# Seven block products in the first chunk's channel product, w_out's first pieces at fixed places, and split weight halves

## The chip, the cores and the metric

The kernel runs on one core of a Trainium2 chip. The metric is the device time of one execution in microseconds (us). The engines are named as the profile names them: PE multiplies matrices, PEld loads its weights, ACT (ScalarE), DVE (VectorE) and POOL (GpSimd) work element by element, SP issues the transfers.

## The reference

Three layers are computed one after the other. The weights come as 64-bit floats, q, k and v as 32-bit ones.

```python
# attention, B 4, H 8, S 576, D 64, window 64
scores = scale * np.matmul(q, k.transpose(0, 1, 3, 2))
mask = (rel >= 0) & (rel < window)
attn = exp(scores - max); attn = attn / (attn.sum + 1e-09)
x = (attn @ v), heads joined: [4, 576, 512]
# gated layer
h = np.maximum(x @ w_in, 0.0)
u, v = (h[..., :512], h[..., 512:])
v_s = np.einsum('ts,bsd->btd', w_spatial, layernorm(v)) + b_spatial[None, :, None]
x = (u * v_s) @ w_out
# mixing layer
h = np.maximum(x.transpose(0, 2, 1) @ w_tok1, 0.0) @ w_tok2
u = x + h.transpose(0, 2, 1)
h2 = np.maximum(u @ w_ch1, 0.0) @ w_ch2      # 512 -> 1536 -> 512
return u + h2
```

## The kernel before

**Number format.** Every product is made of three matmuls on 32-bit words that are split in a high and a low part: high by high, high by low, low by high (`mm3`, L155; the two helpers that make the parts are `split`, L147: a cast on ACT, line L148, and a subtraction, on DVE or POOL, line L149). A 64-bit weight first becomes a 32-bit word: ACT scales its upper half (`down`, L72), and DVE puts the bits together in `to_f32` (L63, then L68 and L69). Words that come by `split_steps` have their cast at L101 and their low part at L103.

**Stages.** First attention and x @ w_in, in 18 steps (n = 0 to 17), written out in a fixed order for all engines (`manual_schedule`). After it the order of the program is chosen by a scheduler from the code's order and from priorities. Behind attention come the spatial product and `wout` (five pieces), `x2nat`, `tok1` and `tok2` (four batches), and between them the preparation of the channel weights: `load_c1(j)` and `load_c2(j)`, j = 0 to 5, each of which turns 128 x 1024 words to high and low parts. Both also make sums of blocks on POOL: `load_c1` writes them to the DRAM tile `sums`, `load_c2` splits its sums and writes all parts to the DRAM tile `scr`. They are put off by priority, and their transfers go out in the order of the list `sources`.

**The channel products.** The 2304 tokens go in three chunks of 768, each as two halves of 384. The first product of a chunk makes the rows j = 0 to 5 of u @ w_ch1 (two blocks of 128 rows, for two halves of tokens). In chunk 0 `ch1` does it plainly: 48 matmuls of 128 x 384 a row, 288 in all, with the casts `uh` and low parts `ul` of u. In chunks 1 and 2 `ch1_seven` takes seven products of half the depth, 42 matmuls a row. These need the four sums of a weight row (read back from `sums`, cast to `sh`, low part `sl`: `load_sums`) and four differences of token blocks t1 to t4 (`usums`, each a DVE subtraction at L771, a cast and a low part, laid in words that are no longer used). The sums of the seven products are put together on DVE (x, z, H) and relu'd on ACT. The second product is seven times `product` (12 matmuls for each of three transferred pieces `w<-scr`). Each takes a cast `oh` on ACT (L898) and a low part `ol` on DVE (L899) for each of its six blocks, and adds its result to U (L936, L947).

Of the kernel before, what the change touches and what calls it, by code (L numbers as in the profile page):

```python
# [10 lines left out]
F32R = mybir.dt.float32r  # L11
# [9 lines left out]
P = 128  # L21
NTOK = B * S
SCALE = 0.125
WN = 256
# [11 lines left out]
def tile_kernel(ctx, tc, qT, kT, kE, v, w_in, wsT, b_sp, w_out, w_t1, w_t2, w_c1, w_c2, outT):  # L36
# [37 lines left out]
    def split_steps(hi, lo, src, rows=P, dup=False, raw=None, val=None, eng=nc.vector):  # L74
# [14 lines left out]
        if wide:  # L89
            r3 = raw[:, :cols].rearrange("p (n w) -> p n w", w=2)  # L90
            low, high = r3[:tot, :, 0], r3[:tot, :, 1]
            if val is None:
                val = stage.tile([P, WN], F32, tag="val", name="val", bufs=2)
            x = val[:tot, :n]
            down(x, high)
            yield
            to_f32(x, [(low, high)])
            yield
        else:
            val = raw  # L100
        nc.scalar.copy(out=hi[:tot], in_=val[:tot, :n])  # L101
        yield
# [356 lines left out]
    def wv_part(k):  # L459
        return w_part(U[:, k, 1152:2176], w_in[128 * k:128 * k + 128, 512:].unsqueeze(1), wi_h[:, k:k + 1, 512:], wi_l[:, k:k + 1, 512:], 512)  # L460

    E = mybir.EngineType
    with tc.manual_schedule(engines={E.PE, E.SP, E.Activation, E.DVE, E.Pool}):
# [61 lines left out]
        uv_v(*its[0])  # L525
        conv, late = {1: (0,), 2: (1, 2), 3: (3,)}, ()
        ws_at = {2: 2, 3: 2, 4: 3, 5: 3}
        for n in range(1, len(its)):
# [10 lines left out]
            go(*cv[:1])  # L539
            go(*cv[:1])  # L540
            if some:
                sexp(n + 1, 0)
                sexp(n + 1, 1)
                snorm(n + 1)
# [14 lines left out]
            while work and left > 0:  # L559
                left -= run_work(1)  # L560
                tick()
            load_ws(ws_at.get(n, 0))
            enable(n)
        while turns:
# [13 lines left out]
    psA = pool("psA", bufs=5, space=PSUM)  # L578
    for k in range(4):
        load_cols(wo_h[:, k, :], wo_l[:, k, :], w_out[128 * k:128 * k + 128, :])  # L580
    while any(w[0] is not spatial for w in work):
# [12 lines left out]
    def c2_source(j):  # L594
# [6 lines left out]
    sources += [(c1_source(j) if w == 1 else c2_source(j), {}) for w, j in  # L601
                ((2, 0), (1, 0), (2, 1), (2, 2), (1, 1), (1, 2), (2, 3), (1, 3), (2, 4), (1, 4), (1, 5), (2, 5))]
    issued = []
# [150 lines left out]
    def usums(c, u):  # L754
# [18 lines left out]
        return [[(h[:, k], l[:, k]) for k in range(2)] for h, l in [(uh[:, :2], ul[:, :2]), (uh[:, 2:], ul[:, 2:]), (vh[:, 2:], vl[:, 2:])] + homes]  # L773

# [30 lines left out]
    tok1(3)  # L805
    load_c2(4)
    tok2(2)
# [29 lines left out]

    def ch1_seven(X):

        x11, x21, x22, t1, t2, t3, t4 = X  # L840
        S = [load_sums(j) for j in range(2)]
        outs, left = [], []
        for j in range(NJ):
            if j and j + 1 < NJ:
                S.append(load_sums(j + 1))
            s1, s2, s3, s4 = S[j]
            a, c = [psmm.tile([P, 512], F32, tag="mm", name="mm")[:, :HW] for _ in range(2)]
# [32 lines left out]
            left = [last]  # L880
            outs.append((h11, h12, h21, h22, e))
        left[0]()
        return [list(x) for x in zip(*outs)]

# [27 lines left out]
    for c in range(NTOK // TW):  # L912
        t0 = TW * c
        u = u[:1] if c == 0 else []
        u += [uin(c, h) for h in range(len(u), 2)]
        if c:
            b11, b12, b21, b22, e = ch1_seven(usums(c, u))
        else:
            b11, b12, b21, b22, e = [], [], [], [], []
            for j in range(NJ):  # L920
                if j == 0:
                    load_c1(5)
                    load_c2(5)
                x, y = ch1(u, j)
                b11.append(x)
                b12.append(y)
                x, y = ch1(u, j + NJ)
                b21.append(x)
                b22.append(y)
                e.append(diff(H(), b12[j], b11[j], nc.vector))  # L930
                diff(b12[j], b22[j], b12[j], nc.vector)
        us = [[U[:, 2 * dh:2 * dh + 2, t0 + HW * h:t0 + HW * h + HW] for h in range(2)] for dh in range(2)]
# [119 lines left out]
```

## Time and profile before

| | |
|---|---|
| median of 3 runs | 638.32 us (637.96 to 638.89) |
| profiled execution | 638.47 us |
| its span | 636.7 us, 12004 instructions |
| PE busy | 610.3 us, 96% of the span |
| DVE, ACT, POOL busy | 459.5, 334.1 and 153.4 us |
| granted clock | 1.00 |

The profiled execution took 1.8 us more than its span, and 0.15 us more than the median. The stages in the trace: attention to about 215 us, then the spatial product, the token mixing and the preparation of weights to 363.5 us, then three chunks, whose first ends near 454 us and whose second near 550 us. A row of the trace gives the start, the duration, the engine, the line, the operation, and in square brackets how long the engine stood idle ahead of it and what ended that.

### The profile page before, as it was taken

What the parts mean: (1) busy time and instruction counts of PE and PEld (TensorE: products, weight loads), DVE (VectorE), ACT (ScalarE), POOL (GpSimd) and SP (SyncE); (2) the same over time, 40 slices, a digit from 0 to 9 for tenths busy, and PEclk for the clock granted to TensorE, in tenths of its full rate; (3) what the DMA queues carried; (4) which work ended last, traced back from release to release, by engine and by line L of the source; (5) the groups of instructions that cost most, each with busy time, mean ns of one, the idle gap of its engine ahead of it and who ended that gap; (6) DMA issues with size and microseconds to landing.
All of it is one profiled execution on the core that took longest, in us unless ns stands there. A gap on an engine that the chain in (4) does not pass through costs nothing.

```text
span 636.7 us, 12004 instructions
## 1 busy us (share of the span) xinstructions
PE 610.3 (96%) x4455; PEld 566.8 (89%) x4455; DVE 459.5 (72%) x977; ACT 334.1 (52%) x839; POOL 153.4 (24%) x166
## 2 busy tenths in 40 slices
PE   5889999999999999999899999999999999999997
PEld 2568798998889899888788899999999999999987
DVE  4896857556584688769978951278875998867982
ACT  4777853545674464666554442345543646344550
POOL 5610000100010010565475471041000440002510
PEclk9999999999999999999999999999999999999999
DMA  8853473222330135557756455057433675534772
GB/s 325 271 158 112 152 235 127 78 77 75 102 116 2 34 118 158 177 193 248 256 183 218 183 174 218 0 198 257 149 125 133 220 230 196 178 103 151 255 248 75
DMA packets 46106, 103.60 MB, mean 163 GB/s; under 512 B 4192, under 2 KB 16736, under 8 KB 46048
## 3 DMA queue, kind: packets, MB, share of 16 engines
q1 hardware_dynamic: 46048, 102.84, 48.3%
q8 instruction: 35, 0.57, 0.4%
q14 instruction: 23, 0.19, 0.1%
HBM read 83.95 MB, written 18.87 MB: 162 GB/s over the span
## 4 chain that ended last, share of the span: by engine, by line
PE 64%; DVE 14%; ACT 7%; DMA 5%; issue 4%; POOL 3%; SPq 1%; DVEq 0%; ACTq 0%; POOLq 0%
PE mm L161 27%; PE A L904 17%; PE mm L833 8%; PE A L833 6%; ACT pb L264 3%; DMA U<-in_w_in 3%; POOL k L738 2%; DVE k L68 2%; DVE k L69 2%; PE xo L297 2%; PE pt L285 2%; DMA scr<-hl 2%; DVE k L63 1%; PE A L161 1%; PE sc L241 1%
## 5 line engine op out<-in xcount | busy, mean ns | idle before, releaser
L904 PE MATMUL A<-oh,w 128*128 128x384 f32 x480 | 102.7, 334 | 0.0
L886 POOL TENSOR_TENSOR H<-H 128x384 f32<-128x384 f32 x36 | 45.0, 1264 | 184.9 <-DVE ol L899 171.0
L899 DVE TENSOR_TENSOR ol<-H,oh 128x384 fp32r<-128x384 f32 x120 | 77.2, 676 | 16.4 <-ACT oh L898 12.7
L904 PEld LDWEIGHTS A<-oh,w 128*128 128x128 f32 x480 | 85.0, 188 | 0.0
L898 ACT CAST oh<-H 128x384 fp32r<-128x384 f32 x120 | 60.0, 514 | 41.5 <-PE A L904 31.0
L904 PE MATMUL A<-ol,w 128*128 128x384 f32 x240 | 61.4, 336 | 2.2 <-DVE ol L899 2.2
L161 PE MATMUL mm<-ws,nh 128*128 128x288 f32 x320 | 62.0, 297 | 0.4 <-DVE tmp L394 0.4
L161 PEld LDWEIGHTS mm<-ws,nh 128*128 128x128 f32 x320 | 49.9, 188 | 1.0 <-DVE tmp L394 0.6
L363 POOL TENSOR_SCALAR rstd<-mv 128x1 f32<-128x1 f32 x18 | 4.9, 272 | 178.4 <-DVE mv L362 178.3
L904 PEld LDWEIGHTS A<-ol,w 128*128 128x128 f32 x240 | 43.1, 188 | 3.3 <-DVE ol L899 3.2
L886 DVE TENSOR_TENSOR H<-H 128x384 f32<-128x384 f32 x36 | 22.6, 628 | 21.8 <-ACT H L826 19.6
L161 PE MATMUL mm<-ws,nl 128*128 128x288 f32 x128 | 37.7, 295 | 0.0
L264 ACT ACTIVATE pb<-pb,nm 128x128 f32<-128x128 f32 x96 | 37.3, 400 | 0.4 <-DVE nm L255 0.4
L286 ACT COPY PT<-pt 128x512 f32<-128x512 f32 x36 | 19.4, 591 | 31.5 <-PE pt L285 31.5
L272 DVE TENSOR_SCALAR rs<-sm 128x8 f32<-128x8 f32 (+1 forms) x19 | 3.3, 172 | 42.9 <-ACT pb L264 42.9
L161 PE MATMUL mm<-xh,wi_h 128*128 128x384 f32 x96 | 32.7, 341 | 0.7 <-ACT vf L357 0.6
L161 PE MATMUL mm<-xh,wi_l 128*128 128x384 f32 x96 | 32.1, 334 | 0.0
L161 PE MATMUL mm<-xl,wi_h 128*128 128x384 f32 x96 | 32.1, 334 | 0.0
L161 PE MATMUL mm<-gh,wo_h 128*128 128x512 f32 (+1 forms) x80 | 29.4, 378 | 0.1
L161 PE MATMUL mm<-gh,wo_l 128*128 128x512 f32 (+1 forms) x80 | 29.4, 370 | 0.0
L161 PE MATMUL mm<-gl,wo_h 128*128 128x512 f32 (+1 forms) x80 | 29.4, 370 | 0.0
L149 POOL TENSOR_TENSOR hl<-k,hl 128x512 fp32r<-128x512 f32 (+1 forms) x24 | 28.6, 1208 | 0.0
(190 smaller groups left out, 1691.4 us busy)
## 6 DMA issues: line engine op xcount, KB each, us to landing
w<-scr SPq DMA_DIRECT2D x63, 512.0 KB, 4.4
k<-in_w_c SPq DMA_DIRECT2D x24, 512.0 KB, 5.3
scr<-hl SPq DMA_DIRECT2D x18, 512.0 KB, 6.1
kk<-in_kT SPq DMA_DIRECT2D x16, 384.0 KB, 4.7
k<-sums SPq DMA_DIRECT2D x12, 512.0 KB, 3.2
qq<-in_qT SPq DMA_DIRECT2D x18, 256.0 KB, 4.0
va<-in_v SPq DMA_DIRECT2D x18, 256.0 KB, 2.9
vb<-in_v SPq DMA_DIRECT2D x18, 256.0 KB, 3.9
```

The lines of the kernel that those rows point to most:

```text
L68: nc.vector.scalar_tensor_tensor(out=y, in0=high, scalar=-0x80000000, in1=y, op0=ALU.bitwise_and, op1=ALU.bitwise_or)
L69: nc.vector.scalar_tensor_tensor(out=y, in0=low, scalar=29, in1=y, op0=ALU.logical_shift_right, op1=ALU.bitwise_or)
L149: eng.tensor_tensor(out=lo, in0=x, in1=f(hi), op=ALU.subtract)
L161: nc.tensor.matmul(o, a, c, start=(i == 0), stop=(i == n - 1))
L264: nc.scalar.activation(out=pb[:, h, :], in_=scs[g][:, h - 4 * g, :] if mk is None else pb[:, h, :], func=AF.Exp, scale=SCALE if mk is None ...
L285: nc.tensor.transpose(pt[:, h, :], pb[:, 4 * g + h, :], ident)
L286: nc.scalar.copy(out=PT[:, 4 * g:4 * g + 4, :], in_=pt)
L833: nc.tensor.matmul(o, a, m, start=first and i == 0, stop=i == len(todo) - 1, skip_group_check=True)
L886: eng.tensor_tensor(out=out, in0=a, in1=b, op=ALU.subtract)
L898: nc.scalar.copy(out=oh, in_=blk[j])
L899: nc.vector.tensor_tensor(out=ol, in0=blk[j], in1=f(oh), op=ALU.subtract)
L904: nc.tensor.matmul(acc[d], a, m, start=(first and j == 0 and i == 0), stop=(last and j == NJ - 1 and i == 2), skip_group_check=True)
```

## The change

It has five parts.

1. The first two of w_out's eight pieces get fixed places in attention: transfers at the end of step n = 11, the scaling on ACT at the end of n = 12, the six DVE operations of both in n = 14. Their casts and low parts, like the other six pieces, stay behind attention. Before, the scheduler placed all of it.
2. `load_c1` makes high and low part of its 1024 columns in two halves of 512.
3. The order of the last weights: all of W_ch1 ahead of W_ch2's fourth and fifth row; `load_c2(4)` and `load_c2(5)` stand in chunk 0 behind its first row, where only `load_c2(5)` stood.
4. `usums` makes t1 and t2 first, and t3 and t4 at a second call; the words in which they lie are exchanged among them.
5. Chunk 0 makes its rows j = 0 and 1 plainly (`ch1_four`), then rows 3, 4, 5 and 2 by seven products. t1 and t2 are made behind row 0; t3 and t4 behind the first two reads of sums. In chunks 1 and 2 the two reads come between t2 and t3.

```diff
+        if callable(hi):
+            hi, lo = hi()
...
+    def wo_part(i):
+        k, c = i // 2, WN * (i % 2)
+        return split_steps(lambda: [w[:, k, c:c + WN] for w in wo], None, w_out[128 * k:128 * k + 128, c:c + WN])
...
+        wo_open = [wo_part(i) for i in range(2)]
...
+            if n == 14:
+                go(*wo_open)
...
+            if n in (11, 12):
+                go(*wo_open)
...
-                ((2, 0), (1, 0), (2, 1), (2, 2), (1, 1), (1, 2), (2, 3), (1, 3), (2, 4), (1, 4), (1, 5), (2, 5))]
+                ((2, 0), (1, 0), (2, 1), (2, 2), (1, 1), (1, 2), (2, 3), (1, 3), (1, 4), (1, 5), (2, 4), (2, 5))]
...
-        split(both[:, :1024], both[:, 1024:], x)
+        for i in (0, 512):
+            split(both[:, i:i + 512], both[:, 1024 + i:1536 + i], x[:, i:i + 512])
...
-        homes = [(thirds(vh[:, :2]), thirds(vl[:, :2])), (apart(0, ws), apart(1, ws)), (apart(0, c1b), apart(1, c1b)),
-                 tuple(thirds(tq.tile([P, 2, HW], F32R, tag=n, name=n)) for n in ("th", "tl"))]
+        homes = [(apart(0, c1b), apart(1, c1b)), tuple(thirds(tq.tile([P, 2, HW], F32R, tag=n, name=n)) for n in ("th", "tl")),
+                 (apart(0, ws), apart(1, ws)), (thirds(vh[:, :2]), thirds(vl[:, :2]))]
...
-        for i, o, a, b in ((0, t1, x12, x11), (1, t2, x22, t1), (2, t3, x22, x12), (3, t4, x21, t2)):
+        for i, o, a, b in ((0, t1, x12, x11), (1, t2, x22, t1)):
...
+        yield
+        for i, o, a, b in ((2, t3, x22, x12), (3, t4, x21, t2)):
...
-    load_c2(4)
...
-    def ch1(u, ft):
+    def ch1(u, j):
...
-        for uh, ul in u:
+        for (uh, ul), ft in [(x, ft) for x in u for ft in (j, j + NJ)]:
...
+    def ch1_four(u, j):
+
+        x, z, y, w = ch1(u, j)
+        e = diff(H(), y, x, nc.vector)
+        return x, diff(y, w, y, nc.vector), z, w, e
+
+    def ch1_all(u, parts, plain):
+
+        outs, left = {}, []
+        seven_js = [j for j in (*range(NJ // 2, NJ), *range(NJ // 2))] if plain else list(range(NJ))
+        seven_js = [j for j in seven_js if j >= plain]
+        for j in range(plain):
+            if j == 0:
+                load_c1(5)
+            else:
+                load_c2(4)
+                load_c2(5)
+            outs[j] = ch1_four(u, j)
+            if j == 0:
+                next(parts)
+        if not plain:
+            next(parts)
+        S = {j: load_sums(j) for j in seven_js[:2]}
+        x11, x21, x22, t1, t2, t3, t4 = next(parts)
...
+        b11, b12, b21, b22, e = ch1_all(u, usums(c, u), 0 if c else 2)
```

What this does to the order of the instructions is seen at three places. In the rows of the order, the number behind L is the line of the kernel whose order it is; the changed kernel's lines from 101 on stand 2 to 38 further down.

**Attention, step n = 14.** DVE, before: vf is the normalised v of an earlier step, rs and pb are the division of the softmax, whose result PE transposes next.

```order
L366 TENSOR_SCALAR vf<-vf,mv,rstd 128x512
L272 TENSOR_SCALAR rs<-sm 128x8
L273 RECIPROCAL rs<-rs 128x8
L274 TENSOR_TENSOR pb<-pb,rs 128x1024
L335 TENSOR_TENSOR nl<-vf,nh 128x512
```

DVE in the changed kernel, at the same place, and below it ACT some steps ahead, where PT is the copy of the transposed softmax that the attention's second product takes (both with `val`, w_out's words).

```order
L368 TENSOR_SCALAR vf<-vf,mv,rstd 128x512
L63 TENSOR_SCALAR val<-val 128x256
L68 SCALAR_TENSOR_TENSOR val<-raw,val 128x256
L69 SCALAR_TENSOR_TENSOR val<-raw,val 128x256
L63 TENSOR_SCALAR val<-val 128x256
L68 SCALAR_TENSOR_TENSOR val<-raw,val 128x256
L69 SCALAR_TENSOR_TENSOR val<-raw,val 128x256
L274 TENSOR_SCALAR rs<-sm 128x8
L275 RECIPROCAL rs<-rs 128x8
L276 TENSOR_TENSOR pb<-pb,rs 128x1024
```

```order
L331 ACTIVATE U<-mm 128x256
L72 ACTIVATE val<-raw 128x256 x2
L288 COPY PT<-pt 128x512 x2
L266 ACTIVATE pb,sm<-pb,nm 128x128 x8
```

The six operations on val have moved in between vf and rs, and the two on ACT in between U and PT; before, both stood some six steps earlier.

**The transfers of chunk 0.** SP, before: `sums<-k` writes the block sums of W_ch1, `scr<-hl` the parts of W_ch2, `w<-scr` reads the weights of the second product.

```order
L717 DMA sums<-k_4583 128x1024
L742 DMA scr<-hl 128x512
L894 DMA w<-scr 128x1024 x3
L742 DMA scr<-hl 128x2x512
L894 DMA w<-scr 128x1024
L742 DMA scr<-hl 128x2x512 x2
L894 DMA w<-scr 128x1024 x13
```

SP in the changed kernel: `k<-sums` reads the block sums back (k_4768 is row j = 3, k_4774 row 4); the first five of the `scr` writes are those of `load_c2(4)` and the start of `load_c2(5)`.

```order
L733 DMA sums<-k_4562 128x1024
L134 DMA k_4652<-in_w_c 128x1024
L134 DMA k_4654<-in_w_c 128x1024
L758 DMA scr<-hl 128x512
L758 DMA scr<-hl 128x2x512 x3
L758 DMA scr<-hl 128x512
L758 DMA scr<-hl 128x2x512
L738 DMA k_4768<-sums 128x1024
L758 DMA scr<-hl 128x2x512 x2
L738 DMA k_4774<-sums 128x1024
L738 DMA k_4843<-sums 128x1024
L932 DMA w<-scr 128x1024 x17
```

The first read of sums has come to stand behind the second `scr` write of `load_c2(5)`, the second read behind its last.

**From the plain rows to the seven products.** ACT in the changed kernel, from the last parts of `load_c2(5)` (k_4677) on: `H<-mm` are the relus of the plain rows, p the copies of a first product, ws the high part of t3 (k_4635).

```order
L150 CAST hl<-k_4677 128x2x256
L845 ACTIVATE H<-mm 128x384 x2
L150 CAST sh<-k_4768 128x1024
L891 COPY p_4799<-mm 128x384
L891 COPY p_4862<-mm 128x384
L900 ACTIVATE H<-mm 128x384
L150 CAST sh<-k_4774 128x1024
L150 CAST ws<-k_4635 128x2x3x128
```

DVE in the changed kernel at the same place: `sl` are low parts of sums, k_4635 and k_4636 are t3 and t4, `ws` is the low part of t3.

```order
L151 TENSOR_TENSOR sl<-k_4768,sh 128x1024
L896 TENSOR_TENSOR x<-A,p_4799 128x384
L898 TENSOR_TENSOR z<-mm,p_4799 128x384
L151 TENSOR_TENSOR sl<-k_4774,sh 128x1024
L791 TENSOR_TENSOR k_4635<-U 128x768
L791 TENSOR_TENSOR k_4636<-U,k_4634 128x768
L896 TENSOR_TENSOR x<-A,p_4862 128x384
L151 TENSOR_TENSOR ws<-k_4635,ws 128x2x3x128
```

PE's rows at this place are 6 matmuls `uh,c1b`, 4 that need `sh`, 12 `uh,c1b`, 8 of which the first needs `sl`, 6 `uh,c1b`, and 18 on the sums of rows 3 and 4, then those on t3. None of these rows stands in the kernel before, where ACT and DVE have the relus and differences of plain rows 2 to 5 here.

## Rows read from the trace of the kernel before

**Rows 1.** PE's waits over the whole span: total us, times, longest.

```profile
PE pt L285 <- DVE pb L274: 5.7, 8, 1.2
...
PE A L904 <- DVE ol L899: 2.2, 3, 1.1
...
PE mm L161 <- ACT U L648: 1.4, 1, 1.4
...
PE mm L161 <- DVE hl L672: 0.7, 1, 0.7
PE mm L161 <- ACT uh L148: 0.7, 1, 0.7
...
PE mm L161 <- DVE U L683: 0.6, 1, 0.6
...
PE mm L161 <- DVE tmp L394: 0.4, 1, 0.4
```

**Rows 2.** Busy time by stretch: chunk 0's first product, chunk 1's.

```profile
364.00:411.70 47.70, 47.70 (x276) 47.67 (x276) 15.21 (x22) 16.50 (x34) 14.47 (x13) 1.00 0.39 138
...
454.00:496.00 42.00, 42.00 (x244) 42.00 (x244) 29.79 (x52) 17.22 (x32) 0.46 (x1) 1.00 0.45 154
```

**Rows 3.** The chain that ended last: start, us, engine, count.

```profile
363.53 48.17 PE mm L161 x276
...
465.09 1.04 PE mm L833 x6
```

**Rows 4.** Timeline of attention: ACT's val pair, steps before and in n = 14.

```profile
90.99 0.78 ACT L72 ACTIVATE val<-raw 128x256 f32<-128x256 f32 x2
...
174.53 1.06 PE L285 MATMUL pt<-ident,pb 128*128 128x128 f32 x8 [0.78 <-DVE pb L274]
...
179.39 0.17 DVE L272 TENSOR_SCALAR rs<-sm 128x8 f32<-128x8 f32 x1 [1.46 <-ACT pb L264]
```

**Rows 5.** Instructions on the tile val: ns minimum, median, maximum.

```profile
L63 DVE TENSOR_SCALAR val<-val x8: 286/293/294, 91.5 to 226.0; 128x256 int32<-128x256 int32 x8
L68 DVE SCALAR_TENSOR_TENSOR val<-raw,val x8: 414/420/427, 93.4 to 227.4; 128x256 int32<-128x256 int32 x8
```

**Rows 6.** Timeline of the stretch before 304.33 us, DVE and ACT.

```profile
301.47 0.68 DVE L69 SCALAR_TENSOR_TENSOR k<-k,k 128x512 int32<-128x512 int32 x1
...
302.19 1.05 ACT L148 CAST ws<-k 128x1024 fp32r<-128x1024 f32 x1 [2.68 <-DVE k L69]
...
303.27 1.52 DVE L149 TENSOR_TENSOR ws<-k,ws 128x1024 fp32r<-128x1024 f32 x1 [0.39 <-ACT ws L148]
...
303.70 0.57 ACT L648 COPY U<-mm 128x512 f32<-128x512 f32 x1
```

**Rows 7.** Timeline of ACT in tok2 of the second batch.

```profile
325.40 1.24 ACT L72 ACTIVATE k<-k 128x512 f32<-128x512 f32 x2 [0.69 <-POOL hl L149]
```

**Rows 8.** Timeline of W_ch2's last row in chunk 0, DVE and POOL.

```profile
368.31 1.28 DVE L69 SCALAR_TENSOR_TENSOR k<-k,k 128x512 int32<-128x512 int32 x2
...
373.69 1.29 POOL L149 TENSOR_TENSOR hl<-k,hl 128x512 fp32r<-128x512 f32 x1
```

**Rows 9.** Transfers of the tile sums, us from issue to landing (minimum, median, maximum).

```profile
DMA to landing us min/median/max: 2.6/3.3/4.6
```

**Rows 10.** POOL's block sums of W_ch2: ns minimum, median, maximum.

```profile
L738 POOL TENSOR_TENSOR k<-k x12: 733/1088/1387, 257.4 to 370.2; 128x256 f32<-128x256 f32 x12
```

**Rows 11.** Groups of instructions from 411 to 520 us: busy us, mean ns of one.

```profile
L149 DVE TENSOR_TENSOR sl<-k,sh 128x1024 fp32r<-128x1024 f32 x6 | 7.3, 1222 | 2.0 <-ACT sh L148 1.7 <-PE mm L833 0.3
L148 ACT CAST sh<-k 128x1024 fp32r<-128x1024 f32 x6 | 6.3, 1053 | 9.4 <-DMA k<-sums 8.1 <-DVE H L886 0.9 <-DVE ol L899 0.4
...
L858 DVE TENSOR_TENSOR x<-A,p 128x384 f32<-128x384 f32 x6 | 3.3, 556 | 4.3 <-ACT p L853 2.3 <-PE A L833 1.9
...
L771 DVE TENSOR_TENSOR k<-U 128x768 f32<-128x768 f32 x2 | 1.9, 954 | 0.2 <-PE A L904 0.2
```

**Rows 12.** Timeline of PE in the second product of chunk 1.

```profile
511.96 0.61 PE L904 MATMUL A<-ol,w 128*128 128x384 f32 x2 [0.76 <-DVE ol L899]
```

More of the change, by code (lines that the diff above doesn't have):

```diff
@@ L460, in wv_part @@
         return w_part(U[:, k, 1152:2176], w_in[128 * k:128 * k + 128, 512:].unsqueeze(1), wi_h[:, k:k + 1, 512:], wi_l[:, k:k + 1, 512:], 512)
+    wo = []
+    def wo_part(i):
+        k, c = i // 2, WN * (i % 2)
+        return split_steps(lambda: [w[:, k, c:c + WN] for w in wo], None, w_out[128 * k:128 * k + 128, c:c + WN])
     E = mybir.EngineType
@@ L578, in tile_kernel @@
     psA = pool("psA", bufs=5, space=PSUM)
-    for k in range(4):
-        load_cols(wo_h[:, k, :], wo_l[:, k, :], w_out[128 * k:128 * k + 128, :])
+    wo += [wo_h, wo_l]
+    for t in wo_open + [wo_part(i) for i in range(2, 8)]:
+        for _ in t:
+            pass
     while any(w[0] is not spatial for w in work):
@@ L765, in apart @@
             return v[:, :, w, 1, :2].rearrange("p j k c -> p k j c")
-        homes = [(thirds(vh[:, :2]), thirds(vl[:, :2])), (apart(0, ws), apart(1, ws)), (apart(0, c1b), apart(1, c1b)),
-                 tuple(thirds(tq.tile([P, 2, HW], F32R, tag=n, name=n)) for n in ("th", "tl"))]
+        homes = [(apart(0, c1b), apart(1, c1b)), tuple(thirds(tq.tile([P, 2, HW], F32R, tag=n, name=n)) for n in ("th", "tl")),
+                 (apart(0, ws), apart(1, ws)), (thirds(vh[:, :2]), thirds(vl[:, :2]))]
         t1, t2, t3, t4 = [k4()[:, :2 * HW].rearrange("p (k c) -> p k c", k=2) for _ in range(4)]
-        for i, o, a, b in ((0, t1, x12, x11), (1, t2, x22, t1), (2, t3, x22, x12), (3, t4, x21, t2)):
+        for i, o, a, b in ((0, t1, x12, x11), (1, t2, x22, t1)):
             nc.vector.tensor_tensor(out=o, in0=a, in1=b, op=ALU.subtract)
             split(*homes[i], thirds(o))
-        return [[(h[:, k], l[:, k]) for k in range(2)] for h, l in [(uh[:, :2], ul[:, :2]), (uh[:, 2:], ul[:, 2:]), (vh[:, 2:], vl[:, 2:])] + homes]
+        yield
+        for i, o, a, b in ((2, t3, x22, x12), (3, t4, x21, t2)):
+            nc.vector.tensor_tensor(out=o, in0=a, in1=b, op=ALU.subtract)
+            split(*homes[i], thirds(o))
+        yield [[(h[:, k], l[:, k]) for k in range(2)] for h, l in [(uh[:, :2], ul[:, :2]), (uh[:, 2:], ul[:, 2:]), (vh[:, 2:], vl[:, 2:])] + homes]
     wout(0)
@@ L836, in H @@
         return Hp.tile([P, HW], F32, tag="H", name="H", bufs=30)
[L838 to L846, printed above, removed]
+    def ch1_four(u, j):
[19 more added lines that the diff above has]
+        x11, x21, x22, t1, t2, t3, t4 = next(parts)
+        for at, j in enumerate(seven_js):
+            if at and at + 1 < len(seven_js):
+                S[seven_js[at + 1]] = load_sums(seven_js[at + 1])
+            s1, s2, s3, s4 = S.pop(j)
             a, c = [psmm.tile([P, 512], F32, tag="mm", name="mm")[:, :HW] for _ in range(2)]
@@ L880, in ch1_seven @@
             left = [last]
-            outs.append((h11, h12, h21, h22, e))
+            outs[j] = (h11, h12, h21, h22, e)
         left[0]()
-        return [list(x) for x in zip(*outs)]
+        return [list(x) for x in zip(*(outs[j] for j in range(NJ)))]
     def diff(out, a, b, eng=nc.gpsimd):
@@ L915, in tile_kernel @@
         u += [uin(c, h) for h in range(len(u), 2)]
[L916 to L931, printed above, removed]
+        b11, b12, b21, b22, e = ch1_all(u, usums(c, u), 0 if c else 2)
         us = [[U[:, 2 * dh:2 * dh + 2, t0 + HW * h:t0 + HW * h + HW] for h in range(2)] for dh in range(2)]
```

## The prediction

> **What bounds the kernel now.** I read the page first (its figures are in the table above): PE is busy for 96% of the span at an undisturbed clock, so the kernel is bound by the number of matmuls, and all that other engines can cost is the few places where PE stands still. The waits of PE [rows 1] list these places; the ones that the change touches are a wait for the softmax's division (pb) in attention, small ones between 304 and 364 us (U, hl, uh), and one for `ol` in the second product of a chunk. The windows [rows 2] then show how far the helpers are from PE: in chunk 0's plain first product DVE works 15.2 of 47.7 us, in chunk 1's, by seven products, 29.8 of 42.0 us. PE has no gap in either. The chain of what ended last [rows 3] gives the price of a matmul: 48.17 us for 276 plain ones, 0.1745 us each, and 1.04 us for six of the seven products, 0.1733 us each.
>
> **The change part by part**, against the profiled execution's 638.47 us; the median of the runs is 638.32, 0.15 us less, and I take that off at the end.
>
> *Fewer matmuls.* Rows 2 to 5 of chunk 0 fall from 48 to 42 matmuls each: 24 x 0.1733 = **-4.16 us**. That is sure, since PE is the bound there and no extra matmul comes in.
>
> *w_out's two pieces in attention.* The ACT pair took 0.78 us [rows 4] and now stands ahead of the PT copies on ACT, behind which the exponentials of the next steps queue; DVE's division waits for these, and PE for the division: it stood 0.78 us at 174.53 [rows 4]. So nothing hides ACT's 0.78 us there but what the chain can give back later; I take 0.7. In n = 14 DVE has an idle stretch of 1.46 us ahead of rs, until ACT's exponentials end [rows 4]. The six operations, at 0.293 and 0.420 us for L63 and L68 [rows 5], and L69 (the same form as L68) at as much, add up to 2.27 us; operations behind each other on DVE overlap a little, so I count 2.0, and rs is 0.5 us late, 0.8 at most. What they leave, near 91 to 98 us, gives back the 0.4 us that PE waited for tmp [rows 1]. Together **+0.8** (from -0.4, if the two delays fall into waits that are there anyway, to +1.2). Behind attention two pieces still have their cast and low part to do; they did before, too.
>
> *W_ch1's parts in halves.* At 302.19 ACT's cast of 1024 columns began when the second L69 had ended (301.47 + 0.68), and DVE waited 0.39 us for it; behind that cast on ACT stands U's copy at 303.70, for which PE waited 1.4 us [rows 1, 6]. The first half needs the first L69 alone and can begin some 0.6 us earlier, so that the second ends some 0.45 us earlier than the whole did, and U's copy with it; the 0.6 us that PE waits for DVE's U [rows 1] shrinks by some 0.35, since the low part ends earlier too. **-0.8** (-0.3 if only U's copy gains part of it, -1.4 if one of the two waits goes whole). At the other five places nobody waits for the whole, and the extra instructions lie beside PE.
>
> *The token products, 318 to 364 us.* In the new order `load_c2(4)` is away from here, and so `load_c1` comes sooner: in the second batch ACT's scaling pair, 1.24 us, which had to wait 0.69 us for POOL to leave a buffer [rows 7], stands ahead of both `hh` and no longer between them. PE waits for hh and I price that at 1.0. Against it the wait for hl, 0.7, goes (its DVE operation had been behind the conversion of the same words), and at the start of chunk 0 the wait for uh, 0.7 [rows 1], since chunk 0's first row now begins with 24 matmuls of the first half of the tokens, 4.2 us, and not with 12, before it needs the second half's cast. In the fourth batch t1, t2 and the words of `load_c2(4)` now stand ahead of `hl` on DVE; the 48 matmuls of the batch before lie between, and I count nothing for it but the upper bound. **-0.5** with 0.1 for smaller waits (-1.5 to +0.8, when this place or another of the waits comes up).
>
> *From plain rows to seven products in chunk 0.* Let T be the end of the last plain matmul. PE goes on with six matmuls of row 3 that need no sums (1.04 us), then it needs `sh`. On ACT the cast of k_4768 stands behind the last plain relu, whose duration I bound by DVE's x of the same size, 0.556; the cast takes 1.053 [rows 11]. So sh is there at T + 1.7 (0.07 us for the hand-over), and PE stands **0.7 us** if the words have landed by T + 0.6. PE then has 48 matmuls until t3's low part is needed: T + 1.7 + 8.4 = T + 10.1. DVE has ahead of it sl 1.222, x and z (0.556 each), sl 1.222, t3 and t4 (0.954 each), x 0.556, and the low part itself, 768 wide like t3, about 0.95 [rows 11]: 7.0 us of work from T + 1.7 on. But x has to wait for the matmuls of its bank (20 behind sh, T + 5.2) and the second x for 44 (T + 9.3). From T + 9.4 on stand x and the low part, 1.5 us, so it is there near T + 10.9, and PE stands **0.7 us** more. To these comes the chance that the words land late; I count 0.1 for it, and treat it below as a rival. **+1.5** (0.9 if the scheduler's low part is less behind than I think, 2.8 with words that land 1.3 us late).
>
> *The second product of chunk 0.* Before, its start had no wait for `ol`. In chunk 1 DVE enters it with work left over from the seven products, and PE stood 0.76 us at 511.96 [rows 12]; three such waits make 2.2 us in all, the longest 1.1 [rows 1], which leaves 1.4 us to chunk 2. Chunk 0 now starts in the same way: **+1.0** (0.5 to 1.5).
>
> *Chunks 1 and 2.* t3 and t4 now come behind two reads of sums. Their work is the same, in another order, and it lies beside the products of the chunk before, but for the last two differences, about 1.9 us each with the low part. I take **+0.2** (-0.5 to +1.0).
>
> Sum: -4.16 + 0.8 - 0.8 - 0.5 + 1.5 + 1.0 + 0.2 = **-2.0**, so 636.5 on the profiled time and **636.4** on the median.
>
> **Rivals.**
>
> *A. The stalls at the seam don't appear.* If sh, t3's low part and `ol` come in time, 2.5 us of the added waits go, and the time is 633.9. For it: PE has no wait within the seven products of chunk 1 [rows 2], although DVE and ACT have the same work there. Against it: chunk 1 makes its sums while the second product of chunk 0 runs, and chunk 0 has no such stretch ahead.
>
> *B. DVE becomes the bound in chunk 0.* In chunk 1 it had 29.8 us of work for six rows [rows 2], 5.0 each: four rows make 19.9, to which t3, t4 and their low parts come, 4 x 0.95 = 3.8, so 23.7 us against 168 x 0.1733 = 29.1 of PE. That fits unless every operation takes 23% longer, or `load_c2(5)`'s conversion slips in behind T. Then it costs up to 2 us, and the time is 638.4: no change.
>
> *C. The sums land late: slower.* On SP the read of k_4768 stands behind the second `scr` write of `load_c2(5)`, which waits for POOL. Before, that part (ending at 373.69 + 1.29 = 374.98) came 5.4 us behind the end of the second L69 (368.31 + 1.28) [rows 8], which was 6.1 us behind the first matmul of the chunk at 363.53 [rows 3]. In the new order the second half's low parts of u and t2's stand ahead of the conversion, so I put its end near 7.1 and the part's near 12.5; if `load_c2(4)`, which POOL must do first, holds it up, 13.5. The read then takes 2.6 to 4.6 us [rows 9]: the words are there 15.1 to 18.1 us after the start. T is 96 x 0.1745 = 16.7 plus small waits, and ACT needs the words at 17.3. The middle is in time; the end is 0.8 us late. Each further us is one of PE. The change is slower by over 0.2% when the words come 3.3 us later than I assume. That needs POOL to work much slower than in the rows; its sums of 128x256 indeed go from 0.733 to 1.387 us [rows 10], and the two rows of W_ch2 that now follow each other are 16 such instructions or larger ones: at 0.35 us more for each, 5.6 us, a good part of which would show. The time is then 638.4 (2 us late) to 640.5 (4 us late). The Trainium skill, page "SBUF — State Buffer", section "Who interferes with whom", says that a DVE instruction with two SBUF inputs contends with a GpSimd instruction that reads SBUF, as an exclusive lock. The spread of POOL's times, next to DVE work with two inputs, agrees with that; the page gives no price, and by it this rival is the likelier the more t1, t2 and low parts fall beside POOL.
>
> *D. The change does less than it says.* The fixed turns may simply take the place of a stretch in which PE waited anyway, and the halves gain nothing: the terms of attention, the halves and the token products then come to +0.5 (1.2, -0.3 and -0.4) instead of -0.5, and the time is 637.4, which is still in the forecast's range; it is most of the 13% below that are not faster.
>
> **How the numbers follow.** What can be told from no change is 0.2%, 1.3 us: faster means below 637.0, slower above 639.6. Forecast with its bounds (the terms' deviations taken as independent, sqrt of the sum of squares, about 2.0 each way): 634.4 to 638.5, 55% (42 of it faster, 13 not). Rival A 17%, faster. Rival B 15%, 2 of it faster, 12 the same, 1 slower. Rival C 13%, 3 the same, 10 slower. Faster 0.61, same 0.28, slower 0.11. The range that leaves out 2 in 10 goes from A's 633.8 to B's and C's lower part, 638.8.
>
> **What would show it.** Right: the first product of chunk 0 has 264 matmuls; PE stands 0.5 to 1.5 us at the first `sh` after the plain rows and at the first `ws,sh`, with ACT `sh` and DVE `ws` as the releasers; a wait for `ol` of 0.5 to 1.5 us some 12 us behind the seven products; the wait for pb near 174 us is 0.5 to 0.8 longer; the one for U at 304 us shorter. Wrong: ACT's `sh` of k_4768 waits for its transfer for more than a us (C); waits on DVE within rows 3 to 2 of more than 2 us (B); no wait at the seam at all (A); waits for `hh` of over 2 us near 325 us.

## The result and the profile after

| | before | changed kernel |
|---|---|---|
| median of 4 runs | 638.14 us | 644.97 us (644.6 to 645.53) |
| profiled execution, span | 638.47, 636.7 us | 644.8, 643.0 us |
| PE busy | 610.3 us | 609.3 us |
| mean granted clock | 1.00 | 0.997 |

The change makes the kernel slower: the ratio is 1.0106, with a 95% interval of 1.0089 to 1.0124, 6.8 us (the two profiled executions differ by 6.3). The forecast was 636.4, with a range that ended at 638.8.

Where the time went is read from four places in the timeline of PE that both kernels have. The first w_out matmul starts at 246.04 before and at 246.10 now; the first matmul of chunk 0 at 360.57 and 363.73; the first of chunk 1 at 454.53 and 460.29; the last matmul ends at 633.27 and 639.63. So 0.1 us was lost up to w_out (0.9 in attention, as will be seen, against a start that happened to be 0.55 us quicker and 0.3 us that came back on the way, at a place not known), 3.1 us in the token products, 2.6 us in chunk 0, and 0.6 us in chunks 1 and 2. Chunk 0 has 24 matmuls fewer and takes longer (PE's count in the whole trace falls from 4455 to 4431).

The waits of PE in the changed kernel, to be held against [rows 1]: total us, times, longest.

```profile
PE pt L287 <- DVE pb L276: 5.8, 6, 1.4
...
PE A L852 <- ACT sh L150: 3.6, 1, 3.6
PE A L942 <- DVE ol L937: 3.4, 5, 1.1
PE mm L163 <- ACT U L663: 2.6, 2, 1.5
PE mm L163 <- ACT hh L686: 2.4, 1, 2.4
...
PE A L163 <- DVE nl L337: 1.0, 1, 1.0
...
PE A L852 <- DVE ws L151: 0.4, 1, 0.4
```

The reader is to see two waits that had no row before: 3.6 us for `sh` at the seam of chunk 0, and 2.4 us for `hh`, which took the place of the 0.7 us for `hl`. The wait for `ol` has grown by 1.2 us, and that for t3's low part (ws) is 0.4 us.

The timeline at the seam, DVE, SP, ACT and PE, ordered by their start; the first matmul of the chunk began at 363.73.

```profile
364.94 3.34 DVE L151 TENSOR_TENSOR ul<-U,uh 128x768 fp32r<-128x768 f32 x2
368.20 2.05 DVE L151 TENSOR_TENSOR tl<-k,th 128x768 fp32r<-128x768 f32 x1
370.17 1.78 DVE L63 TENSOR_SCALAR k<-k 128x1024 int32<-128x1024 int32 x1
373.20 1.29 DVE L69 SCALAR_TENSOR_TENSOR k<-k,k 128x512 int32<-128x512 int32 x2
377.77 1.28 POOL L151 TENSOR_TENSOR hl<-k,hl 128x512 fp32r<-128x512 f32 x1
379.60 0.34 SPq L738 DMA_DIRECT2D k<-sums  x1
384.04 1.04 ACT L150 CAST sh<-k 128x1024 fp32r<-128x1024 f32 x1 [2.87 <-issue]
385.13 0.69 PE L852 MATMUL A<-th,sh 128*128 128x384 f32 x1 [3.56 <-ACT sh L150]
```

The conversion of `load_c2(5)` ended at 374.49, 10.8 us behind the chunk's first matmul; the second part was through POOL at 379.05, 15.3 us behind it, the read of sums went out at 379.60, and the cast on it began at 384.04, 20.3 us behind the first matmul. The last plain matmul ended near 380.5. ACT's row names no releaser for its idle 2.87 us; that it is the transfer is what the first experiment tells. These 2.87 us are the lateness of the words; the other 0.7 of PE's 3.56 us would have been there with words in time, since the cast stands behind the last plain relus, which ended at 381.17.

What came behind the stall is in the windows of PE: us, busy (instructions), granted clock, DMA share, GB/s.

```profile
383.00:384.00 1.00, 0.00 (x0) 1.00 1.02 399
384.00:385.00 1.00, 0.00 (x0) 0.96 1.05 397
385.00:386.00 1.00, 0.86 (x3) 0.50 1.16 346
386.00:387.00 1.00, 1.00 (x5) 0.50 0.91 365
387.00:388.00 1.00, 1.00 (x5) 0.50 0.38 152
388.00:389.00 1.00, 1.00 (x7) 0.83 0.00 0
389.00:390.00 1.00, 1.00 (x8) 1.00 0.00 0
```

PE had stood still for 3.56 us and then worked at 0.50 of its clock (1.2 instead of 2.4 GHz) for 3.2 us: half of that, 1.6 us, is lost on top of the stall.

The stall for hh, ACT and PE, the place of [rows 7]:

```profile
325.93 1.21 ACT L72 ACTIVATE k<-k 128x512 f32<-128x512 f32 x2
327.16 1.09 ACT L686 ACTIVATE hh<-A 128x512 fp32r<-128x512 f32 x2
327.81 0.40 PE L163 MATMUL mm<-t_h,hh 128*128 128x288 f32 x1 [2.38 <-ACT hh L686]
```

Both scaling operations stand ahead of both hh; before, the first hh had gone at 324.11, ahead of the pair.

### The profile page after: what moved, and what is told of

The parts are those of the page before. It is cut to its first block, busy times and chain, and to the rows that moved or that the text cites. A ratio compares the mean times of both kernels' runs of the same rounds, so it can differ in the third digit from the quotient of the medians.

```text
span 643.0 us, 12044 instructions
## 1 busy us (share of the span) xinstructions
PE 609.3 (95%) x4431; PEld 565.0 (88%) x4431; DVE 491.7 (76%) x1015; ACT 342.5 (53%) x857; POOL 154.2 (24%) x166
## 4 chain that ended last, share of the span: by engine, by line
PE 61%; DVE 18%; ACT 6%; issue 5%; DMA 5%; POOL 4%; SPq 1%; DVEq 0%; ACTq 0%; POOLq 0%
PE mm L163 19%; PE A L942 17%; PE mm L852 10%; PE A L852 8%; POOL k L754 2%; DVE k L68 2%; ACT pb L266 2%; DMA kk<-in_kT 2%; DVE k L69 2%; PE xo L299 2%; DVE k L63 2%; PE sc L243 2%; PE pt L287 2%; DMA scr<-hl 2%; DVE U L698 1%
## 5 line engine op out<-in xcount | busy, mean ns | idle before, releaser
L924 POOL TENSOR_TENSOR H<-H 128x384 f32<-128x384 f32 x36 | 43.7, 1233 | 187.8 <-DVE ol L937 187.8
L942 PE MATMUL A<-ol,w 128*128 128x384 f32 x240 | 62.9, 337 | 3.4 <-DVE ol L937 3.4
L924 DVE TENSOR_TENSOR H<-H 128x384 f32<-128x384 f32 x36 | 26.5, 736 | 8.2 <-ACT H L845 4.3
L151 POOL TENSOR_TENSOR hl<-k,hl 128x512 fp32r<-128x512 f32 (+1 forms) x24 | 30.7, 1290 | 0.0
```

The lines of the kernel that those rows point to most:

```text
L151: eng.tensor_tensor(out=lo, in0=x, in1=f(hi), op=ALU.subtract)
L924: eng.tensor_tensor(out=out, in0=a, in1=b, op=ALU.subtract)
L942: nc.tensor.matmul(acc[d], a, m, start=(first and j == 0 and i == 0), stop=(last and j == NJ - 1 and i == 2), skip_group_check=True)
```

## The experiments

The medians of the kernel before are those of the runs on the same chip.

### The place of the first read of sums

`sums_ahead` is the changed kernel with this edit:

```diff
             else:
                 load_c2(4)
-                load_c2(5)
...
-        S = {j: load_sums(j) for j in seven_js[:2]}
+        S = {seven_js[0]: load_sums(seven_js[0])}
+        if plain:
+            load_c2(5)
+        S[seven_js[1]] = load_sums(seven_js[1])
```

> The changed kernel, but the first read of block sums (row 3) stands ahead of load_c2(5) in the program and so on SP. Theory (the words land late): in the changed kernel PE stood 3.55 us for sh and then worked at clock 0.50 for some 3.5 us; of the stall about 2.9 us is lateness of the words, and the low clock costs about 1.7 us more. With the read ahead, the stall should fall to 0.5 to 1.0 us, the clock stay at 1.00, and the time fall by 4 to 5 us, to 640 to 641. Rival (ACT's order: sh stands behind the last plain relus anyway): the stall stays near 3 us and the time near 645.

Measured: 642.72 us against 638.53, 2.2 us less than the changed kernel, not 4 to 5. The read went out at 368.90, the cast began at 372.41 after waiting 2.42 us for the transfer, and PE had no wait for row 3's sh at all, only 0.28 us for sl and 0.43 for ws. Between the first matmuls of chunk 0 and chunk 1 lie 92.2 us instead of 96.6: in the chunk the gain is 4.3 us, as expected, and the theory holds. The read and the cast in this kernel, to be held against 379.60 and 384.04 above (the chunk's first matmul began at 365.14):

```profile
368.90 0.32 SPq L738 DMA_DIRECT2D k<-sums  x1
372.41 1.05 ACT L150 CAST sh<-k 128x1024 fp32r<-128x1024 f32 x1 [2.42 <-DMA k<-sums]
```

What was missing in the total is elsewhere; these are its windows behind the stall for hh, which is 2.38 us here too:

```profile
328.00:329.00 1.00, 0.57 (x2) 0.62 0.78 202
329.00:330.00 1.00, 1.00 (x6) 0.50 1.07 374
330.00:331.00 1.00, 1.00 (x7) 0.50 1.06 412
331.00:332.00 1.00, 1.00 (x7) 0.68 0.96 332
332.00:333.00 1.00, 1.00 (x9) 1.00 1.08 379
```

In the changed kernel's own profile the clock had stayed at 1.00 behind that stall; here it fell. So a stall of this length costs 2.4 us in some executions and about 1.6 more in others.

### The place of load_c2(4)

```diff
+    load_c2(4)
     tok2(2)
...
-                ... (2, 3), (1, 3), (1, 4), (1, 5), (2, 4), (2, 5)
+                ... (2, 3), (1, 3), (2, 4), (1, 4), (1, 5), (2, 5)
...
             else:
-                load_c2(4)
                 load_c2(5)
```

> The changed kernel with load_c2(4) back where it stood before (ahead of tok2 of the third batch, and in the old place of the list of sources). Theory (POOL's work on load_c2(4) stretched DVE's ul and tl, from 1.9 to 3.3 and from 0.95 to 2.1 us, and so made load_c2(5) and the read of sums late): ul, tl take 0.95 each again, the stall for sh falls from 3.55 to about 1 us, the clock stays at 1.00, and the time falls by 3 to 5 us. The stalls between 320 and 360 us (2.4 for hh, 1.0 for nl) go back to the 0.7 of before, 2 us more: 638 to 640 in all. Rival (load_c2(5) alone is late enough, and the stalls at 320 to 360 come from the halves): the time stays within 1 us of 645.

Measured: 644.7 us (642.9 to 646.73), no different. Half of the theory holds: ul take 1.81 us for the pair and tl 0.94 again, now that POOL is idle beside them. But the words come no sooner. In this execution the chunk's first matmul began at 364.62; the conversion of `load_c2(5)` ended at 374.43, 9.8 us behind it instead of 10.8, since DVE has U's additions and c1's second half ahead of ul instead, and the cast on the words began at 385.16, 20.5 us behind it instead of 20.3 (ACT's row names the transfer here, 3.63 us). The stall for sh falls from 3.56 to 2.13 us all the same, because PE comes to the place later: it waited 1.38 us for DVE's U in the plain rows. The clock still falls (0.85 from 380 to 390 us), PE waits 3.0 us for DVE's U in all, and the stall for hh stays at 2.3 us. So POOL's neighbourhood made the low parts slow, but taking it away did not bring the words sooner; and the stall for hh does not come of this move.

### The halves

`no_halves` is the changed kernel with

```diff
-        for i in (0, 512):
-            split(both[:, i:i + 512], both[:, 1024 + i:1536 + i], x[:, i:i + 512])
+        split(both[:, :1024], both[:, 1024:], x)
```

> The changed kernel with load_c1's 1024 columns split in one piece, as before. Theory (the halves are worth little; the second wait for U, 1.5 us at 307 us, came of a transfer of weights that landed late): the time stays within 0.7 us of 645. Rival (the halves put more instructions ahead of hh, nl and U on ACT and DVE, and the 2.9 us that the stretch from 300 to 364 us lost are theirs): 2 to 3 us faster, 642 to 643.

Measured: 645.48 us, no different in sum. Its waits of PE between 300 and 430 us:

```profile
PE mm L851 <- ACT p L890: 2.1, 1, 2.1
PE A L851 <- ACT sh L150: 2.1, 1, 2.1
PE mm L163 <- ACT U L663: 1.4, 1, 1.4
PE A L163 <- DVE U L698: 1.3, 1, 1.3
PE mm L163 <- DVE hl L687: 0.8, 1, 0.8
```

The wait for hh is gone and that of before, 0.8 us for hl, is back: the halves made it. (The wait for hh stands in the profiles of all six kernels of this study that have the halves, 2.3 to 2.4 us, and in none of the other eight.) But a new order also makes the seam worse, by a wait for p, which stands on ACT behind the parts of `load_c2(5)`. The time alone would have said that the halves do nothing; the next kernel has them by themselves.

`halves_only` is the kernel before with the same edit the other way round, and nothing else:

> The kernel before with nothing changed but load_c1's split in two halves. In its order both scaling operations (L72) stand ahead of both hh of the second batch on ACT, as in the changed kernel; with one piece one hh stands between them. Theory (the halves turn that order round and so make the stall at 328 us): PE waits 2.4 us for hh there instead of 0.7 for hl, the waits for U at 304 to 310 us change by less than 0.7 us together, and the time is 1 to 3 us longer than before, the upper end if the clock falls after the stall. Rival (my prediction: the halves bring U's copy forward, and the order at 328 us comes of the moved load_c2(4)): 0.5 to 1 us faster than before, and no wait for hh.

Measured: 640.55 us (638.37 to 643.37) against 638.03, a ratio of 1.0037 (1.0021 to 1.0053), 2.4 us slower. PE's waits from 300 to 360 us:

```profile
PE mm L161 <- ACT hh L671: 2.4, 1, 2.4
PE mm L161 <- ACT U L648: 1.4, 2, 1.0
PE mm L161 <- DVE U L683: 1.2, 2, 0.9
```

The theory holds. U's copy does come sooner, as I had said: the wait at 304 us falls from 1.42 to 1.04. But the waits behind it grow, and the waits for U together are longer than before, 2.6 us against 2.0 ([rows 1]: 1.4 and 0.6). The wide spread of the ten runs goes with the clock: the four with a mean granted clock of 0.999 or more took 638.4 to 639.7 us, the six with 0.994 to 0.997 took 640.4 to 643.4. That the fall in these six lay behind this stall is not shown; in the profiled run, one of the four, it stayed at 1.00 there.

### The fixed turns

`no_turns` is the changed kernel with

```diff
-            if n == 14:
-                go(*wo_open)
...
-            if n in (11, 12):
-                go(*wo_open)
```

> The changed kernel with w_out's first two pieces left to the scheduler, as before. Theory: the two waits for pb near 174 and 181 us are 0.78 and 0.72 again instead of 1.35 and 1.44, and the wait of 0.37 near 98 us is back: 0.9 us faster, 644. Rival (the waits are made up for later, since attention ends at the same time): no difference, within 0.3 us.

Measured: 645.15 us (644.26 to 646.27): no difference that shows in the time, although the waits for pb in its profile are back at 0.77 and 0.71 us, and the 0.34 for tmp, too. Its own seam stall is 3.9 us, and its clock falls twice. So this run tells nothing on 0.9 us, and the turns were tried alone: `turns_only` is the kernel before with these four lines, `wo_part` and the list of pieces behind attention.

> The kernel before with nothing changed but the fixed turns of w_out's first two pieces. Theory: the waits for pb near 174 and 181 us grow from 0.78 and 0.72 to 1.35 and 1.43, that of 0.34 near 98 us goes: 0.9 us slower. Rival (what is lost there comes back behind attention): within 0.3 us of before.

Measured: 638.75 us against 638.14, 1.0013 (1.0001 to 1.0025), 0.6 to 0.8 us slower; the interval only just leaves out no difference. The two waits, to be held against 174.53 in [rows 4]:

```profile
173.14 1.07 PE L287 MATMUL pt<-ident,pb 128*128 128x128 f32 x8 [1.35 <-DVE pb L276]
180.51 1.07 PE L287 MATMUL pt<-ident,pb 128*128 128x128 f32 x8 [1.41 <-DVE pb L276]
```

### The seven products alone, and with the read ahead

`seven_only` is the changed kernel without turns, halves and moved rows of W_ch2 (`load_c2(5)` in row 0). `seven_ahead` is the same with `load_c2(5)` behind the first read of sums, by the edit of `sums_ahead`. Against the changed kernel, besides the three edits above:

```diff
             if j == 0:
                 load_c1(5)
+                load_c2(5)
-            else:
-                load_c2(4)
-                load_c2(5)
```

> The changed kernel without the fixed turns, the halves and the moved rows of W_ch2: of the change only the seven products in chunk 0 with t1, t2 first are left, and load_c2(5) stands in row 0 as before. Theory (24 matmuls are worth 4.2 us; the words of sums come late by what load_c2(5) on DVE and POOL needs, about 2 us as with load_c2(4) back): a stall of 1 to 2.5 us for sh, 1.2 us for ol, 0.3 in chunk 1, and 0 to 1.7 us by a lower clock: 636 to 639. Rival (the seam alone eats the gain whole, as load_c2(5) has t1 and t2 ahead of it on DVE): a stall of over 4 us and 640 or more.

Measured: 637.92 us (637.09 to 641.21) against 638.03, 1.0008 (0.9992 to 1.0024): the same. The stall for sh is 1.28 us, those for ol 1.16, and the clock stays at 1.00. The stall has the length that I expected, but not the cause. The read stands behind two `scr` writes of `load_c2(5)` here, too, yet with that row in the plain row j = 0 it went out 13.0 us behind the chunk's first matmul (359.56), not 15.9, and ACT had no idle time ahead of the cast: it stood behind t2's cast `th`, which waited for DVE.

```profile
372.56 0.41 SPq L733 DMA_DIRECT2D k<-sums  x1
377.47 0.83 ACT L150 CAST th<-k 128x768 fp32r<-128x768 f32 x1 [1.14 <-DVE k L782]
378.60 1.04 ACT L150 CAST sh<-k 128x1024 fp32r<-128x1024 f32 x1
```

> The same as seven_only, but with the first read of sums ahead of load_c2(5). Theory: the stall at the seam is below 1.2 us in all, the clock stays at 1.00, and the time is -4.2 + 1.0 + 1.2 + 0.3 against before, 636 to 637. Rival (what waits at the seam is not the transfer, but DVE's low parts): the seam still takes over 2 us, and the time is that of seven_only.

Measured: 637.11 us (635.85 to 637.84), 0.9982 (0.9972 to 0.9991): 0.9 to 1.2 us faster than before, the only kernel of this study that is, and faster than the change by 7.9. Its waits of PE from 300 to 430 us:

```profile
PE mm L163 <- ACT U L659: 1.9, 2, 1.3
PE A L938 <- DVE ol L933: 1.2, 2, 0.8
PE mm L163 <- DVE ul L151: 0.9, 1, 0.9
PE mm L163 <- DVE hl L683: 0.7, 1, 0.7
PE A L848 <- DVE ws L151: 0.4, 1, 0.4
```

The seam is down to the 0.4 us for t3's low part. Chunk 0 takes 92.65 us from its first matmul to that of chunk 1, 1.3 less than before, and chunks 1 and 2 take 0.6 more, as in all kernels with the new order of t1 to t4. So the theory holds to a few tenths.

### The moved rows of W_ch2, without turns and halves

`ahead_plainrest` is `sums_ahead` with the edits of `no_halves` and `no_turns`.

> The changed kernel without the fixed turns and the halves, with the first read of sums ahead of load_c2(5); against seven_ahead it differs only in that W_ch2's fourth row stands in chunk 0, as the change has it. Theory (the move of load_c2(4) costs by itself nothing once the read is ahead, or gains the waits it took from 340 to 354 us): within 0.7 us of seven_ahead. Rival (POOL's work beside ul and tl still delays DVE's low parts): 1.5 us or more slower than seven_ahead, with waits for DVE at the seam.

Measured: 645.24 us, 1.0111: 8 us slower than seven_ahead. That is the rival's side, but not its cause: PE waits for ACT at the seam, and for DVE only ahead of the chunk (the third row, at 356.47). Its waits of PE:

```profile
PE A L847 <- ACT sh L150: 2.8, 1, 2.8
...
PE mm L847 <- ACT p L888: 1.6, 1, 1.6
PE A L163 <- DVE U L694: 1.3, 1, 1.3
```

The read of row 3 went out at 370.48, in time; that of row 4 only at 386.08, behind `load_c2(5)`'s writes, and p stood on ACT behind a cast that waited for POOL. POOL worked at `load_c2(4)` until 372.5 and came to `load_c2(5)` at 380.33. The clock is 0.66 from 390 to 400 us. So here moving one read only moved the stall to the next wait. It need not be so: `sums_ahead` has the same two rows in the same cover, and no wait of more than 0.43 us at the seam. There POOL came to `load_c2(5)` 13.2 us behind the chunk's first matmul, here 17.8. The two kernels differ in the turns and the halves alone, so it is the order that the scheduler picked that decided, and which difference turned it was not tried. The move by itself, `c2_only`, is on the kernel before:

```diff
-    load_c2(4)
     tok2(2)
...
                 if j == 0:
                     load_c1(5)
-                    load_c2(5)
+                if j == 1:
+                    load_c2(4)
+                    load_c2(5)
```

> The kernel before with nothing changed but the place of W_ch2's last rows: load_c2(4) in chunk 0 behind row 0, load_c2(5) after it, and the list of sources in that order. Theory (the move only puts work beside PE and costs where somebody waits for it; with plain rows nobody needs sums): the wait of 1.3 us for U near 357 us that two kernels with the move and without halves show, against 0.7 for uh that goes; within 1 us of before. Rival (the move makes the plain rows or the second product wait by itself): over 1.5 us slower.

Measured: 637.84 us against 638.14, 0.9992 (0.9981 to 1.0003), the same; no wait of PE in the plain rows, and the wait of 1.3 us near 357 us that I had expected is not there. The move costs nothing where nobody waits for sums.

### What the clock costs

`fill` is the changed kernel with five matmuls more:

```diff
+            if plain and at == 0:
+                w = outs[plain - 1][3]
+                for _ in range(5):
+                    nc.tensor.matmul(b, w[:, :128], w, start=True, stop=True)
             seven(b, s2, t2, True)
```

> The changed kernel with five matmuls that nobody needs (on the last plain block, into the bank that the next product overwrites) put ahead of the first one that needs sh, so that PE works in most of the stall there. It leaves nothing out. Theory (the stall costs twice: 3.6 us of standing, and the fall of the clock to 0.50 after it, some 1.7 us): the stall falls to below 1 us, sh comes at the same time, the clock stays at 1.00 between 380 and 392 us, and the time falls by 1.2 to 1.8 us. Rival (the low clock is a matter of chance or of the rest of the program): the clock falls all the same and the time is within 0.5 us of the changed kernel's.

Measured: 644.0 us (643.53 to 645.63), 1.0 less than the changed kernel, a little under the lower end, and not clear of the noise of so few runs (against the kernel before the ratios are 1.0097, 1.0081 to 1.0113, and 1.0106, 1.0089 to 1.0124). In the profiles chunk 0 takes 95.8 us instead of 96.6. PE's windows around the place, where PE's first matmul on sh began at 386.77, 21.5 us behind the chunk's first, as in the changed kernel (21.4):

```profile
382.00:384.00 2.00, 2.00 (x11) 1.00 1.10 293
384.00:386.00 2.00, 2.00 (x8) 1.00 0.92 359
386.00:388.00 2.00, 1.56 (x9) 1.00 1.07 382
388.00:390.00 2.00, 2.00 (x13) 1.00 0.43 176
```

The five matmuls (ten rows in the trace) took 3.39 us in the place of the stall, 0.44 us of waiting is left, and the clock stays at 1.00 through the whole stretch. The mean granted clocks of all runs fit: it is 0.999 or 1.00 in four of fill's six and 0.994 to 0.997 in all four of the changed kernel's. So the fall is a consequence of standing still. Two waits of 0.26 and 0.97 us behind it, which the changed kernel did not have, took a part back.

### One plain row

`plain_one` is seven_ahead with one plain row:

```diff
-        b11, b12, b21, b22, e = ch1_all(u, usums(c, u), 0 if c else 2)
+        b11, b12, b21, b22, e = ch1_all(u, usums(c, u), 0 if c else 1)
```

> seven_ahead with one plain row and five by seven products: six matmuls fewer, 1.0 us. Theory (what counts at the seam is when the sums and the low parts are there; with one row less of cover, 8.3 us, they come late): stalls of 3 us or more at the seam, and perhaps a lower clock: 2 to 5 us slower than seven_ahead. Rival (the seam is short enough): 0.5 to 1 us faster than seven_ahead, 636.

Measured: 644.93 us, 1.0107: 7.8 us slower than seven_ahead, more than expected. PE waits 6.8 us for sh, and the clock is at 0.67 from 380 to 390 us. Six matmuls saved stand against a row of cover of 8.3 us that is missing.

## Why the prediction was wrong, point by point

**Fewer matmuls, -4.16.** Right: chunk 0 has 264 matmuls. With the seam in order, chunk 0 is 1.3 us shorter (seven_ahead). Waits eat 1.8 of the rest: 1.2 for ol, 0.4 for ws, 0.2 more for ul than before for uh; the remaining 1.0 is in none of PE's waits, and where it went is not known.

**w_out's pieces, +0.8.** Right in mechanism and size: 1.35 and 1.41 us for pb instead of 0.78 and 0.72, and turns_only is slower by 0.6 to 0.8, with an interval that only just leaves out 0.

**The halves, -0.8.** Wrong, in sign. The step that failed is "At the other five places nobody waits for the whole, and the extra instructions lie beside PE". What I missed is that a smaller piece changes the order that the scheduler picks for everything else: both L72 came to stand ahead of hh. I had seen that order, but in **the token products** I put it down to the moved `load_c2(4)`, and priced it at 1.0, against gains that were to outweigh it. It is 2.4 us, its cause is the halves (no_halves, halves_only, c2_back), and the halves as a whole cost 2.4 us in the kernel before. The wait for uh went, as I had said. The wait of 1.0 for nl at 346 us, for which I had only the upper bound, came up as well; it lies between 0.3 and 1.1 in all seven kernels in which `load_c2(4)` stands in chunk 0, and is in none of the other seven; what sets its length was not tried.

**The seam, +1.5.** This is the step that failed with the largest amount: "so I put its end near 7.1 and the part's near 12.5" and with it "The middle is in time". Measured from the chunk's first matmul, the conversion ended at 10.8, the part at 15.3, and the words were on hand at 20.3 and not at 16.6: rival C, to which I gave 13%, with its lateness of 3.3 us just reached. Of the stall 2.9 us are this lateness, and 0.7 is what the sum had. The low part of t3 was 0.4 late and not 0.7.

The working began at a wrong row. "which was 6.1 us behind the first matmul of the chunk at 363.53" takes the chain's 276 matmuls for the chunk's beginning. The chunk has 288, and twelve ran ahead of the wait for uh:

```profile
360.57 0.34 PE L161 MATMUL mm<-uh,ws 128*128 128x384 f32 x1
363.53 0.62 PE L161 MATMUL mm<-uh,ws 128*128 128x384 f32 x2 [0.70 <-ACT uh L148]
```

So in the kernel before the conversion ended 9.0 us behind the first matmul, and the same working then gives 10.0 for the conversion, 15.4 for the part, and 18.0 to 21.0 for the words, where ACT needs them at 17.3: late by 0.7 to 3.7. The lateness would then have stood in the sum, and not among the rivals. That 10.0 and 15.4 come so close is luck in part. DVE reached ul 1.2 us behind the first matmul and not 4.3, which I had not foreseen, and lost 3.2 us again, since ul, tl and L63 took 3.34, 2.05 and 1.78 us, where the same widths took 1.81 and 0.94 in c2_back and 1.23 in the kernel before.

The Trainium skill, page "SBUF — State Buffer", section "Who interferes with whom", has a rule on this, a DVE instruction with two SBUF inputs against POOL's reads; ul and tl are of this kind, POOL worked beside them without a break, and in c2_back, where POOL was idle then, they took 0.9 each: the traces agree. DVE is not always the one that loses time: in no_halves and ahead_plainrest ul and tl took 0.9 each beside a busy POOL, and two of POOL's sums took 4.13 us, where one alone takes 0.73.

That slowness alone was not the cause, since in c2_back the words came no sooner. Two things had to come together: the read of sums stood behind that row's writes on SP (ahead of them it is in time, sums_ahead and seven_ahead), and the row itself was prepared late (in seven_only the read stands behind the same two writes, but the row is prepared in the first plain row, and the words are not waited for).

**The clock.** No step of mine had it: I read a granted clock of 1.00 in the trace of before and took it as given. Every stall that I priced at its length costs more if PE's clock falls after it: 1.6 us here by the windows. That the fall comes of the stall is shown by fill; that its time comes back whole is not.

**ol, +1.0, and chunks 1 and 2, +0.2.** 1.2 us (0.35 and 0.84) and 0.6 us: both nearly right. Half of the latter is a new wait of 0.34 us for p in chunk 1.

**The sum.** Against -2.0: up to chunk 0 the halves and the token products are off by 3.7 us (+3.1 instead of -0.6, as the 0.7 for uh lies in chunk 0 and was right), the seam by 2.5 (4.0 instead of 1.5), the clock by 1.6, the rest by 0.6, less 0.55 of a quicker start and 0.3 in attention; that is 7.6, and the profiled execution came out 8.3 us above the 636.5 of the sum. The 0.7 us that are missing lie in chunk 0 and stay unexplained. No rival had this size: C's own times ended at 640.5, since each us late was one us of PE there. Two of the signs that I had named for being wrong came, the cast's wait for its transfer and the wait for hh of over 2 us.

**What stays open.** Which of the new order's small differences turned the scheduler's choice at 325 us, beyond that the halves do it; why the same two rows of W_ch2 in chunk 0 leave the seam in order in sums_ahead and not in ahead_plainrest; and why the clock fell behind the stall of 2.4 us in three profiled executions (sums_ahead, c2_back, no_turns) and not in three others (the changed kernel, halves_only, fill).

## What to carry to other kernels

Where work is taken off the engine that bounds the kernel, what is needed at the new seam must be followed back through every queue, transfers too: one row of saved matmuls is worth 1 us, and here a read that stood behind the writes of a row prepared late cost 4. In a kernel whose order a scheduler picks, an edit that looks local (a copy in two halves) is judged by what it does to the order of the instructions that others wait for, and is tried alone: the halves by themselves cost 2.4 us, more than twice what the seven products gained with their read moved ahead. Undoing one part of a change can tell nothing, when another part's stall takes up what it frees. Adding one part to the kernel before told the price of the halves and of the turns, but not all: the move of `load_c2(4)` costs nothing there (c2_only) and 8 us beside the seven products (ahead_plainrest against seven_ahead).

## What was not expected of the hardware

After PE stood still for 2.1 us or more (up to 6.8) in chunk 0, its granted clock fell, during the stall or shortly behind it, in all six profiled executions in which that happened. It read 0.50 for some 3 us in the changed kernel, where the mean of the whole execution still read 0.997, and for 6 to 7 us in plain_one, which stood for 6.8 us, and in no_halves and ahead_plainrest, which have two stalls close together. After waits of up to 1.5 us between 60 and 630 us it stayed at 1.00. In six of the fourteen profiled executions the clock also read 0.83 between 10 and 20 us, at the start of attention; w_out began within 1.4 us of its time of before in all of them.
